# Recurrent attention and a two-layer mixer on one core: the last batch's u transposed by TensorE, and a new group order

## The chip, the cores and the metric

One core of a Trainium2 chip. The metric is device time in microseconds (us), the median of five runs. A separate profiled execution gives the trace; its times are microseconds from the start of its span. The engines are called PE or TensorE (matmul; PEld is its weight load), DVE or VectorE, ACT or ScalarE, POOL or GpSimd, and SP or SyncE. A "q" after an engine's name (ACTq, SPq) is its sequencer, which issues DMAs.

## The reference

Four batches, eight heads of 48, 768 steps, all in float32. First a gated linear recurrence, then a mixer along the sequence with rank 32 and a two-layer MLP (384 to 1536 to 384):

```python
for t in range(S):
    state = alpha[:, :, t, :, None] * state + einsum('bhd,bhe->bhde', k[:, :, t], v[:, :, t])
    y[:, :, t] = einsum('bhd,bhde->bhe', q[:, :, t], state)
x = y.transpose(0, 2, 1, 3).reshape(B, S, H * D)
h = x.transpose(0, 2, 1) @ U @ V          # along the sequence, rank 32
u = x + h.transpose(0, 2, 1)
out = u + maximum(u @ w_ch1, 0) @ w_ch2
```

## The kernel before, in words

Each batch is cut into six chunks of 128 steps. The kernel holds four kinds of work for a batch, in this order of dependence.

*The attention of a chunk.* alpha, k, q and v are loaded by SyncE's queue (L370 for batches 0 and 1, L377 for 2 and 3). ScalarE takes the log (lt, L400 or L583). TensorE sums it along the steps (L415 to L424, or L590 and L592). ScalarE makes the exponentials aa and ai (L431, L432, L600, L601) and tot. VectorE or GpSimd multiplies: rk = k times ai, rq = q times aa (L446, L612). Both are transposed to kt and qt. In batches 0 to 2 TensorE does it through PSUM (L459, L632) with a copy by ScalarE (L324) or VectorE (L326). In batch 3 a DMA transpose on ScalarE's queue does it (L623), 12 of them: the set TRD names batch 3's six chunks. TensorE then makes the scores (L486, L653), VectorE masks them (pm, L497, L663), and TensorE adds the state's part and the chunk's part (L560 and L567, or L710 and L712) to a bank that is copied to xb. A state st is carried from chunk to chunk (L518 or L676, then L545 or L699 and L531 or L687). Batches 0 and 1 (PAIR) use another split of heads and steps, in six units of the same kind.

*The mixer.* utx is xb against U for all six chunks (L727), copied once. Each chunk then gets one matmul against V (L758), and VectorE adds xb to it: ub (L759). For the first layer, u must stand transposed, as uT. Batch 0 (XT) builds it on TensorE from xb directly (L746, L749). Batches 1 and 2 transpose ub on TensorE, two chunks and six 128x128 tiles at a time (L774), and VectorE or ScalarE copies the bank to uT. Batch 3 (the tuple TRU) instead issues one DMA transpose per chunk on ScalarE's queue (L763).

*The first layer* (mlp1): for each half of the sequence and each of 12 column groups, three 128x384 matmuls (L801) and a ReLU copy to h1t by ScalarE (L811) or VectorE (L813).

*The second layer* (mlp2): for each chunk, 12 matmuls in three groups of four (L831), the sum with u on VectorE (L843), and the store by SyncE (L848).

*The order.* Nothing runs where it is written. Every step is recorded as an operation with its possible engines, its cost on each, what it reads and what it writes; 1035 in all. The long string TABLE then lists the operations by number, with a letter where an engine is chosen (P, A, V, G). `place` walks through TABLE with a model of the engines' clocks and gives out the buffers, and `run` emits the operations in that order, so each engine's queue is TABLE's order cut down to its own operations. In the head, `run` adds matmuls on a filler tile (L317) where the model has TensorE idle. An operation of mode "X" is a DMA transpose; `place` gives it a landing time, which is one of the two constants that the diff touches:

```python
if op.mode == "X":
    clock[eng] = t + cost
    end[op] = t + (4300.0 if dma > t + 800.0 else 2700.0) - self.LAT[eng]
    dma = max(dma, t) + 300.0
```

These numbers are not seen by the hardware. They matter for which buffer an operation gets and for the filler count.

Buffers come from pools: 36 for loads (io), three for kt, four for qt, three for uT, four for the stored rows (ou), and eight PSUM banks. All DMAs, the loads and stores of SyncE's queue and the transposes of ScalarE's queue, share eight completion semaphores in turn, so a DMA is not issued before an earlier one with the same semaphore has landed.

Of the kernel before, what the change touches and what calls it, by code (L numbers as in the profile page):

```python
# [39 lines left out]
class Plan:  # L40
# [47 lines left out]
    def place(self, table):  # L88

        names = {"P": "PE", "A": "ACT", "V": "DVE", "G": "POOL", "S": "SP"}  # L90
        self.order = []
        clock = dict(self.BEGIN)
        dma = port = 0.0
        mode = "F"
        end = {}
        lanes = []
        for x in table.split():
            op = self.ops[int(x.rstrip("PAVGS"))]
            eng = op.eng = names[x[-1]] if x[-1] in names else next(iter(op.engs))
            cost = op.engs[eng]  # L100
            t = clock.get(eng, 0.0)
            for d in op.deps:
                t = max(t, end[d] + (0.0 if eng == d.eng == "PE" else self.LAT[d.eng]))
            for b in op.bufs:
                if b.slot is None:
                    free = b.pool.free
                    at, b.idx = min((f, n) for n, f in enumerate(free) if f is not None)
                    b.slot = b.pool.slots[b.idx]
                    free[b.idx] = None
                    t = max(t, at)  # L110
            if eng == "POOL":
                t = max(t, port)
            if eng == "DVE" and op.port:
                t = max(t, port - self.PORT)
            queued = eng == "SP" or op.mode == "X"
            if queued and len(lanes) >= 8:
                t = max(t, lanes[-8])
            op.t = t
            if op.mode == "X":
                clock[eng] = t + cost  # L120
                end[op] = t + (4300.0 if dma > t + 800.0 else 2700.0) - self.LAT[eng]
                dma = max(dma, t) + 300.0
            elif eng == "SP":
                dma = max(dma, t + 500.0) + cost
                clock[eng] = max(t + 450.0, dma - 2300.0)
                end[op] = dma + (600.0 if op.deps else 1200.0)
            else:
                if eng == "PE" and op.mode != mode:
                    cost += self.SWITCH
                    mode = op.mode  # L130
                clock[eng] = end[op] = t + cost
                if eng == "POOL" or (eng == "DVE" and op.port):
                    port = end[op]
            if queued:
                lanes.append(end[op] + self.LAT[eng])
            for b in op.bufs:
                b.left -= 1
                b.last = max(b.last, end[op] + self.LAT[eng])
                if b.left == 0:
                    b.pool.free[b.idx] = b.last  # L140
            self.order.append(op)
        self.clock = clock
# [14 lines left out]


TABLE = """
61 69 73 201 224 157 204 160 65 62 64 63 179 66 182 227 161 162 206 184 183 67 164G 158G 165V 186G 1 159A 205 163 71 167 166 70 68 187V 169V 209G 188  # L160
189 168A 230 190A 191A 180A 207 170 173 171 174 172 74 72 192 211 4 181G 208G 228 77 202G 231G 75 81 78 213A 229 185 194 76 195 175 210 176 203A 212V
177 178A 247 214 233 193 196 235A 197 217 218 250 268 215 251 232G 252 79 254G 216 198 234 199 271 236V 200V 219 82 80 83 84 6 85 225G 237 253 226A 272
273 256 220 274 258A 93 5 19 89 21 23 255V 275G 240 257 221 3 248G 259A 241 222 239 242 238 25 27 31 277 260 29 33 35 91 13 17 249A 279A 86 51 97 87
263 88 15 276V 243 278 264 270A 269G 2 261 8 7G 20G 244 280A 245 284 262 285 265 286 22G 281 388 246A 90 39 92 43 37 41 95 282 24G 9 11 432 223A 266
283 267V 391 287 26G 45 10V 394 288A 53 94 49 295 292 298 392 393 410 12V 289 290 304 435 307 291V 305 299 293 296 30G 301 101 47 294V 436 300A 308
297A 302 96 413 306A 32A 28A 415 414 318 316 36G 418G 34G 309V 303V 342 343A 344 322 326 327A 323V 345V 416 319A 59 57 105 55 103 99 320 324 340 346
332 325V 347V 321V 395G 18G 348 328 354 352 438 437 341A 100 14A 98 102 106 356 353A 455 349V 317V 355V 329V 396V 417G 330 420 397 399V 350 16A 331A
422A 107 398 389G 411G 390G 0 336 314 315A 337V 357V 400A 351A 104 310 419 338 421V 311V 339V 312 334 404 38A 333A 40A 42A 423 401 313V 109 424 405 406
402 403 108 110 412G 426 44G 458 460 461 52A 335A 50G 113 368 358 363 427 478 408 373 425 440V 428 439G 111 459 46A 48A 481 434G 429G 430 359 409V 482
433A 431A 483 484 58A 499 56A 54A 407G 60G 442 369 448 441 449 374 364 502 444V 443V 450G 486G 451 463V 457G 504 503 462G 360 445 446 361 465 370 488  # L170
365 456A 485V 447 505 467A 490A 506G 471 487 464 453 508 366 489V 371 117 372 115 112 491 466A 507G 468 118 114 119 472 454A 493 509 473G 375 479A 510A
480G 494 452G 511A 618 474 470 495 500A 378 512 469 620 501G 621 475V 492 515 379 476 637 622 496G 497 516 624G 514 513 498A 626 517G 639 518 625V 627
477V 380 641 623 519A 640 642 116 520 125 120 367 127 134 129 121 130 123 122 126 133 145 135 628V 629V 630 381 383 631 632 124 521A 657 524 528 530
384 522 659 619G 644G 643G 661 662 525 531 534 385 536 523 660 526 664G 638G 663G 658G 529 532 535 537 633 646 645 538 533V 527A 554 552 386 648A 539V
582 666 647A 553V 668A 584 558 570 652 555V 634 583V 559V 585V 665 540 132 131 141 137 387 128 653 541V 580 560 544 545V 376 667A 377 153 142 581A 571A
697 649 669 671 561V 546 548 562 670 651 650 549A 572 677 566 586 547A 563A 574 699 654V 567V 587A 717 679 564 672 550 702 680 565A 700 701 551V 683V
673 576 542 681 577A 578 556 573V 557V 575V 568 685 655 719 675 832 569V 676V 682 543A 674G 684G 703G 834 579A 836 635 686 603 720 835 837 721 687A 604
636V 704V 723V 656V 839G 678G 598 599 706 705 605 725 724G 838G 707V 727V 722 688A 708A 709 689 841 867 711 710 691 606 726 600 593 692 698G 728A 849
840 693 690 601 149 382 602 136 147 729 588 851 869 870 872 885 138 146 589 712 139 694G 731 713 695 594 595 715 730 714G 871 696A 718A 732 590 716V
733V 842 843 873G 591 844 734 607 921 887 608 903 735A 853 744 742 738 609 743 745 890 889 852 833A 750 875 888 751 739 892G 748 610 746 749 855G 891G  # L180
613 856G 736 752 611 140 592 747V 753V 143 905 847 614 845 794 615 894 906 893 908 858 737 907 850A 740 846 795V 874G 741V 848V 596 784 800 758 759V
616 785V 151 150 801V 854 857 754 923 862 780 790 768 796 755A 925 876 863 781V 797A 778 772 791A 779V 773V 769V 764 760 788 864G 910G 909V 765V 924
761A 926 756 144 155 154 148 152 757A 912 789V 868G 877 895 859 896 878 879 897 766 762 927V 860 798 767A 763A 880 886G 881 928V 911 929 861 802 883
803 770 898 786 792 882G 904G 799A 930 771A 884A 793V 899 787V 900V 774 865 807 776 916 782 866A 777A 775V 783A 917 362 617 156 913 931 914 915 901 817
902A 812 933 932 919 818 922G 918G 934 827 920A 935A 828 936 804 937A 944 941 945 805 942 813 950 946 808 938 953 951 939 819 943 940 947 822 823 814
824 954 948 806 612 597 952 955 829 809 949 962 970 956 830 815 825 968 960 972 820 963V 958 964 969A 957V 965A 986 990 984 816 831 821 987V 991V 959A
985A 961V 976 810 982 983A 971A 994 978 992 996 979A 973V 966 980 981V 988 967V 977A 989A 974 1004 997V 1002 975V 1003A 998 1019 1024 1000 1005 995A
993V 1001A 999A 1020 1021 1006 1014 1025 1015 1009 1026 1016 1007 1022 1010 1011 1023 1008 826 1027 1017 1029 811 1028 1012 1032 1018 1013 1030 1031
1033 1034
"""  # L190


# [5 lines left out]
def kernel(  # L198
# [31 lines left out]

    PAIR = (0, 1)
    TRD = {(3, c) for c in range(NC)}
    TRU = (3,)
    XT = (0,)
    P = Plan()
    nc.scalar.preload_act_table_set("natural_log_exp_and_others")
# [148 lines left out]
    def xk(b, xb, c):  # L385
        return [(xb, c, 0), (xb, c, 1)] if b in PAIR else [(xb, c)]
# [334 lines left out]
    def stage_mix(b, xb, ub, uT):  # L721
# [34 lines left out]
        for c in range(NC):  # L756
            hb = Buf(bank)
            P.add({"PE": mm(DM)}, lambda e, c=c, hb=hb: nc.tensor.matmul(hb()[:, 0:DM], lhsT=vm_sb[:, c * C : (c + 1) * C], rhs=utx(), start=True, stop=True), r=[utx, ("vm", c // NT)], w=[hb])  # L758
            P.add({"DVE": 465}, lambda e, c=c, hb=hb: nc.vector.tensor_tensor(ub()[:, c, :], xb()[:, c, :], hb()[:, 0:DM], op=ALU.add), r=[hb] + xk(b, xb, c), w=[(ub, c)])  # L759
            if b in TRU:  # L760
                P.add(
# [141 lines left out]
```

## Time and profile before

| | before |
|---|---|
| runs (us) | 164.51, 163.67, 163.83, 164.35, 163.97 |
| median | 163.97 |
| profiled execution: its time, its span | 164.51, 162.7 |
| granted TensorE clock, mean | 1.00 |
| busy us: PE, weight loads, DVE, ACT, POOL | 153.1, 101.4, 117.1, 92.4, 60.2 |
| first L801 (first layer of batch 0) issued at | 28.62 us |
| DMA transposes: q of batch 3, median to landing | 6 of 4.6 us |
| DMA transposes: k of batch 3, median to landing | 6 of 3.6 us |
| DMA transposes: u of batch 3, median to landing | 6 of 3.1 us |
| TensorE's transposes of u in batches 1 and 2 (L774) | 36, no idle time before them |

A busy time is the union of an engine's instructions. A matmul's end is modelled and lies behind its stream of columns, so two matmuls that follow each other overlap in the rows; what a matmul costs is the distance from its start to the next one's. In the chain of work that ended last each piece is cut to the time in which it held up the rest. In a row of a timeline, "x30" is a run of 30 equal instructions, with its first start and the time to its last end.

### The profile page before, as it was taken

The numbers are of one execution on the slowest core, as the hardware profiler recorded it, in microseconds if no ns is written. First come the engines' busy times: TensorE is split into PE (matmuls) and PEld (weight loads), VectorE is DVE, ScalarE is ACT, GpSimd is POOL, SyncE is SP. The second block draws the span as 40 slices with busy tenths as digits, with TensorE's granted clock in tenths as the row PEclk, the third lists the DMA queues.
The fourth block names the chain that finished last, engine by engine and source line by source line (L and its number), as shares of the span: only waits on it lengthen the run. The fifth ranks groups of instructions, "written<-read, shape, count | busy, mean of one in ns | idle before, by whom it ended". The sixth has DMA issues, their size and how long they took to land.

```text
span 162.7 us, 4418 instructions
## 1 busy us (share of the span) xinstructions
PE 153.1 (94%) x1663; PEld 101.4 (62%) x1663; DVE 117.1 (72%) x255; ACT 92.4 (57%) x232; POOL 60.2 (37%) x94
## 2 busy tenths in 40 slices
PE   7789989999999999999999999997999997999992
PEld 2446867666676876765677666664657564666662
DVE  6379997486947998988798979887995437443241
ACT  4798999758798767635977465453353100453000
POOL 3197654538348675500078246332241000000000
PEclk9999999999999999999999999999999999999999
DMA  5999899999999898998997569999920097200072
GB/s 125 285 292 277 215 278 291 334 256 342 360 273 266 174 227 164 235 197 165 208 229 149 131 154 240 254 177 187 237 53 0 0 163 209 69 0 0 12 283 98
DMA packets 92198, 30.97 MB, mean 190 GB/s; under 512 B 85872, under 2 KB 92144, under 8 KB 92176
## 3 DMA queue, kind: packets, MB, share of 16 engines
q1 hardware_dynamic: 83152, 28.52, 72.3%
q10 hardware_dynamic: 9024, 2.16, 7.6%
q8 instruction: 13, 0.21, 0.5%
q14 instruction: 9, 0.07, 0.2%
HBM read 23.79 MB, written 4.72 MB: 175 GB/s over the span
## 4 chain that ended last, share of the span: by engine, by line
PE 73%; DMA 13%; SPq 6%; ACT 2%; issue 2%; DVE 2%; POOL 1%; DVEq 0%; POOLq 0%; ACTq 0%
PE ps L831 25%; PE ps L801 25%; DMA qt<-rq 6%; SPq L370 6%; DMA io<-in_k_dram 4%; DMA uT<-ub 3%; PE ps L653 2%; PE ps L632 2%; PE ps L459 2%; PE ps L567 2%; PE ps L486 1%; PE ps L712 1%; PE ps L758 1%; PE ps L590 1%; PE ps L774 1%
## 5 line engine op out<-in xcount | busy, mean ns | idle before, releaser
L831 PE MATMUL ps<-w_sb,h1t 128*128 128x384 bf16 (+2 forms) x300 | 53.7, 319 | 0.0
L801 PE MATMUL ps<-uT,w_sb 128*128 128x384 bf16 x288 | 50.2, 326 | 1.1 <-DMA uT<-ub 1.1
L811 ACT ACTIVATE h1t<-ps 128x384 bf16<-128x384 f32 x44 | 20.8, 496 | 31.3 <-PE ps L801 20.8
L801 PEld LDWEIGHTS <-w_sb 128*128 128x128 bf16 x288 | 27.2, 98 | 18.1 <-issue 1.5
L831 PEld LDWEIGHTS <-h1t 128*128 128x128 bf16 x300 | 27.0, 97 | 14.7 <-issue 0.3
L813 DVE TENSOR_SCALAR h1t<-ps 128x384 bf16<-128x384 f32 x52 | 26.8, 552 | 12.0 <-PE ps L801 12.0
L843 DVE TENSOR_TENSOR ou<-ub,ps 128x384 f32<-128x384 bf16 (+2 forms) x19 | 9.7, 528 | 11.4 <-PE ps L831 11.3
L497 DVE TENSOR_TENSOR pm<-ps,maskp 128x512 bf16<-128x512 f32 x24 | 15.9, 682 | 1.7 <-PE ps L486 0.8
L663 DVE TENSOR_TENSOR pm<-ps,maskc 128x512 bf16<-128x512 f32 x24 | 15.5, 684 | 2.0 <-PE ps L653 1.6
L687 POOL TENSOR_TENSOR st<-sm,tot 128x384 bf16<-128x384 f32 x6 | 5.2, 870 | 24.1 <-DMA io<-in_q_dram 12.4
L446 POOL TENSOR_TENSOR rk<-io,ai 128x384 bf16<-128x384 f32 x11 | 10.1, 926 | 10.0 <-DMA io<-in_v_dram 4.9
L759 DVE TENSOR_TENSOR ub<-xb,ps 128x384 bf16<-128x384 bf16 x18 | 8.8, 548 | 4.2 <-PE ps L758 4.2
L612 POOL TENSOR_TENSOR rq<-io,aa 128x384 bf16<-128x384 f32 x9 | 8.5, 949 | 8.5 <-ACT aa L601 5.8
L324 ACT COPY qt<-ps 128x512 bf16<-128x512 bf16 x14 | 9.6, 687 | 2.0 <-PE ps L632 1.1
L600 ACT ACTIVATE ai<-ps 128x384 bf16<-128x384 f32 x12 | 5.9, 501 | 5.0 <-PE ps L592 4.2
L324 ACT CAST xb<-ps 128x384 bf16<-128x384 f32 x14 | 6.6, 478 | 3.5 <-PE ps L712 1.7
L328 POOL CAST rw<-io 64x384 bf16<-64x384 f32 x14 | 7.7, 556 | 1.7 <-DMA io<-in_v_dram 0.9
L601 ACT ACTIVATE aa<-ps 128x384 bf16<-128x384 f32 x12 | 5.8, 497 | 3.8 <-DVE ub L759 1.7
L612 POOL TENSOR_TENSOR rk<-io,ai 128x384 bf16<-128x384 f32 x8 | 7.3, 916 | 1.9 <-PE ps L653 1.1
L328 POOL CAST w_sb<-io 128x384 bf16<-128x384 f32 x11 | 5.5, 505 | 6.2 <-DMA io<-in_moe_w_ch_dram 6.1
L400 ACT ACTIVATE lt<-io 128x384 bf16<-128x384 f32 x12 | 6.2, 525 | 2.4 <-DMA io<-in_alpha_dram 2.3
L446 DVE TENSOR_TENSOR rq<-io,aa 128x384 bf16<-128x384 f32 x7 | 4.8, 691 | 3.3 <-DMA io<-in_q_dram 3.2
(124 smaller groups left out, 259.6 us busy)
## 6 DMA issues: line engine op xcount, KB each, us to landing
io<-in_alpha_dram SPq DMA_DIRECT2D x24, 192.0 KB, 3.9
io<-in_k_dram SPq DMA_DIRECT2D x24, 192.0 KB, 4.5
io<-in_v_dram SPq DMA_DIRECT2D x24, 192.0 KB, 4.1
io<-in_q_dram SPq DMA_DIRECT2D x24, 192.0 KB, 4.4
io<-in_moe_w_ch_dram SPq DMA_DIRECT2D x24, 192.0 KB, 4.5
out_dram<-ou SPq DMA_DIRECT2D x23, 192.0 KB, 2.9
out_dram<-ou SPq DMA_DIRECT2D x1, 128.0 KB, 1.7
v_in<-in_moe_V_dram SPq DMA_DIRECT2D x1, 96.0 KB, 3.5
```

The lines of the kernel that those rows point to most:

```text
L324: nc.scalar.copy(dst, src)
L328: nc.gpsimd.tensor_copy(dst, src)
L370: lambda e: nc.sync.dma_start(t().rearrange("p (h j) d -> p h (j d)", j=2), src[b, hs, sl, :].rearrange("h (p j) d -> p h (j d)", j=2)),
L446: eng.tensor_tensor(jh(dst()[:, :, 0:D]), raw(a), jh(x()), op=ALU.mult)
L497: nc.vector.tensor_tensor(dst, s2, maskp.to_broadcast([C, 2, 2, C]), op=ALU.mult)
L612: eng.tensor_tensor(dst()[:, :, 0:D], a(), x(), op=ALU.mult)
L663: nc.vector.tensor_tensor(pm()[:, :, par, :], s2, maskc.to_broadcast([C, HP, C]), op=ALU.mult)
L801: nc.tensor.matmul(hb()[:, 0:TW], lhsT=w1_sb[:, ct, jt * 128 : (jt + 1) * 128], rhs=uT()[:, ct, tt * TW : (tt + 1) * TW], start=(ct == 0), ...
L811: nc.scalar.activation(dst, hb()[:, 0:TW], AF.Relu)
L813: nc.vector.tensor_scalar_max(dst, hb()[:, 0:TW], 0.0)
L831: nc.tensor.matmul(hb()[:, 0 : hi - lo], lhsT=h1()[:, jt, c * C : (c + 1) * C], rhs=w2_sb[:, jt, lo:hi], start=(jt == 0), stop=(jt == NJ - ...
L843: nc.vector.tensor_tensor(ou()[:, lo:hi], base()[:, c, lo:hi], hb()[:, 0 : hi - lo], op=ALU.add)
```

## The change

Three places change. TRU becomes empty, so batch 3's u takes the same path as that of batches 1 and 2: three groups of six TensorE transposes and three copies from PSUM in place of six DMA transposes. The number of operations stays 1035. The landing times that `place` gives a DMA transpose are longer. And TABLE is another order throughout, from the first load on, with other engines chosen for many copies and products. The 12 DMA transposes of batch 3's q and k stay on ScalarE's queue.

```diff
-                end[op] = t + (4300.0 if dma > t + 800.0 else 2700.0) - self.LAT[eng]
+                end[op] = t + (5000.0 if dma > t + 800.0 else 3800.0) - self.LAT[eng]
...
 TABLE = """
-61 69 73 201 224 157 204 160 65 62 64 63 179 66 182 227 161 162 206 184 183 67 164G 158G 165V 186G 1 159A 205 163 71 167 166 70 68 187V 169V 209G 188
...
-1033 1034
+69 65 61 201 157 179 63 64 62 160 204 162 165V 73 66 67 71 77 159A 161 164G 158G 167 182 169V 184 163 206 183 207 224 205 75 166 173 70 168V 186V 174
...
+1034
 """
...
     TRD = {(3, c) for c in range(NC)}
-    TRU = (3,)
+    TRU = ()
     XT = (0,)
```

The order's effect on single engines, counted in the instruction lists of the two kernels: VectorE takes 59 of the 96 h1t copies (52 before), 11 of the kt copies from PSUM (8), 7 of the qt copies (4), three more of the st products of batches 1 and 2, 11 of the uT copies (8); ScalarE makes one of the two vm copies and batch 0's utx copy. In batch 3 ScalarE's transposes come in the order of chunks 0, 2, 1 and 3 mixed, 5, 4; before it was 0, one of 2, 3, 1, the other of 2, 4, 5.

## The prediction

> **What bounds the kernel now.** I read the page first, for shares; then busy time by windows, for who is full where; then TensorE's waits and the chain, for what stops it; then TensorE's timeline at those stops.
>
> ```profile
> span 162.7 us, 4418 instructions
> ...
> PE 153.1 (94%) x1663; PEld 101.4 (62%) x1663; DVE 117.1 (72%) x255; ACT 92.4 (57%) x232; POOL 60.2 (37%) x94
> ```
>
> The same, by windows (PE, weight loads, DVE, ACT, POOL, granted clock, DMA share, GB/s):
>
> ```profile
> 28.60:108.00 79.40, 79.38 (x908) 53.97 (x907) 66.29 (x133) 54.14 (x144) 38.55 (x55) 1.00 0.99 228
> 108.00:113.50 5.50, 4.46 (x47) 2.75 (x45) 3.85 (x9) 2.54 (x7) 2.41 (x3) 1.00 1.20 180
> 113.50:122.50 9.00, 8.49 (x97) 5.48 (x92) 8.63 (x17) 3.69 (x8) 3.30 (x5) 1.00 0.68 142
> 122.50:131.00 8.50, 8.50 (x88) 5.26 (x86) 4.32 (x9) 1.91 (x4) 0.00 (x0) 1.00 0.09 21
> 131.00:136.20 5.20, 4.10 (x26) 2.32 (x25) 2.53 (x6) 0.00 (x0) 0.00 (x0) 1.00 0.95 158
> 136.20:159.80 23.60, 23.54 (x156) 14.68 (x156) 9.26 (x19) 5.83 (x13) 0.00 (x0) 1.00 0.28 93
> ```
>
> From 28.6 us, the first matmul of the first MLP layer, TensorE is full except around 112, 122 and 136 us. Its waits and the chain name the same culprit, DMA transposes:
>
> ```profile
> PE ps L653 <- DMA qt<-rq: 1.6, 2, 1.0
> PE ps L801 <- DMA uT<-ub: 1.1, 1, 1.1
> ```
>
> ```profile
> 106.76 5.88 DMA qt<-rq
> 112.77 0.85 PE ps L653 x24
> ...
> 117.97 4.05 DMA qt<-rq
> 122.16 0.40 PE ps L653 x8
> ...
> 131.63 4.38 DMA uT<-ub
> 136.15 0.97 PE ps L801 x5
> ```
>
> A matmul's end is modelled late, so I count issue to issue; the chain's merged rows give 0.162 us for a 128x384 matmul (0.49 for three). Then:
>
> ```profile
> 106.69 5.04 PE L801 MATMUL ps<-uT,w_sb 128*128 128x384 bf16 x30
> 121.25 0.40 PE L653 MATMUL ps<-qt,kt 48*128 48x128 bf16 x8
> 130.98 4.06 PE L831 MATMUL ps<-w_sb,h1t 128*128 128x384 bf16 x24
> ```
>
> Thirty matmuls fill 4.86 us, to 111.55; the next starts at 112.77: 1.2 lost. The eight score matmuls fill 0.19, to 121.44; the next start at 122.16: 0.7 lost. Twenty-four fill 3.89, to 134.87; the next starts at 136.15: 1.3 lost. Together **3.2 us**. That is all the change can win after 28.6 us, save 0.15 us at each return from a score group to full-width matmuls (24 score matmuls hold TensorE 0.85 us in the chain, 8 hold 0.40).
>
> **Part 1: batch 3's u by TensorE.** Six DMA transposes leave ScalarE's queue (issued 129.00 to 137.11, landing after 2.4 to 5.4 us); three groups of six TensorE transposes and three evictions come. The rows for this in batches 1 and 2 are "PE ps L774", 0.34 us for six and 0.67 for twelve: 18 cost **+1.0 us**, all on the path since TensorE is full there. The three evictions (0.55 us on VectorE twice, 0.80 on ScalarE once) should be covered. I follow the tightest hand-over in the changed order. L758 of chunk 2 is issued; its sum on VectorE starts 0.36 us later (128.06 to 128.42 in the trace) and lasts 0.55, so it is there after 0.91. TensorE meanwhile has L758 itself (0.16), four L831 (0.65) and the transposes of chunks 0 and 1 (0.34), so it asks for that sum after 1.15. The transposes of chunks 2 and 3 then take 0.34, a matmul's tail about 0.16, the eviction 0.55: uT is there after 1.05, while TensorE does those transposes, one L758 and four L831 (1.15). L801 starts with 0.1 to spare, and the 1.3 us wait goes. If this cover fails by one VectorE instruction, it costs 0.5. SyncE's later stores reused the semaphores of the six transfers; they have until the end and gain nothing.
>
> The Trainium skill speaks against this part: "TensorE: Matmul & The Clock Gate", Part 4, gives a 128x128 TensorE transpose about 275 ns in one kernel's context; by that figure 18 would cost an estimated 4.95 us, and the sum below would come out 2.9 us above the kernel before. The rows above give 56 ns from issue to issue, at a granted clock of 1.00, and the measurement decides.
>
> **Part 2: q and k of batch 3 stay 12 DMA transposes on ScalarE's queue; the new order places their users later.** Landings in the loaded stretch (97 to 112 us) took 4.13, 4.54, 4.11, 4.76, 6.28 and 5.88 us. Before, the score group of chunks 1 to 3 waited for chunk 2's q, loaded last and transposed at 106.76. In the new order ScalarE waits for chunk 0's result (L712), copies it (0.48) and issues the last four at 1.2 us each, so the last is issued about 4.4 us after that L712. TensorE has 18 groups of L801 (0.49 each), one L676 and one L590/L592 in that interval, 9.2 us: 4.8 remain to land. Four of six rows fit, two miss by 1.1 and 1.5: I take **0.4** (0 to 1.5) instead of 1.2. Of chunks 4 and 5 the last transpose waits for a qt buffer that chunk 1's L710 reads last; from there to its scores TensorE has six groups of L831 and 1.1 us of small groups, 5.0, against a flight of 4.05 at that place before: 0 to 0.5, I take **0.1** instead of 0.7. Behind that wait on ScalarE stand the xb copies of chunks 2 and 1, which TensorE needs only for L727. Loads can stand behind a transpose too: a load or store reuses the semaphore of an earlier transfer, and "SPq L848 <- DMA qt<-rq" is 3.0 us in SyncE's waits. In the new order it is chunk 1's k and q loads that wait for chunk 0's two transposes; all loads for the first score group still come before ScalarE reaches their transposes, by my stepping some 2 us. One return from scores fewer in the order: **-0.15**.
>
> **Part 3: the head.** The same work stands before the first L801 in both orders, but VectorE gets three more kt copies (0.42), one more rk product (0.69), one more xb copy (0.55), one qt copy fewer (0.73): +1.9 us, and it is full there:
>
> ```profile
> 12.00:16.00 4.00, 3.66 (x66) 2.56 (x65) 3.88 (x9) 3.48 (x10) 3.28 (x5) 1.00 1.04 275
> 16.00:20.00 4.00, 3.77 (x72) 3.23 (x70) 3.89 (x9) 3.83 (x11) 2.15 (x3) 1.00 0.86 222
> 20.00:24.00 4.00, 3.58 (x78) 2.70 (x76) 4.00 (x10) 3.88 (x8) 2.65 (x7) 1.00 1.06 274
> ```
>
> Against it: its first product waited until 8.18 us for a q loaded seventh; that q is now fourth, and its aa (1.3 us after a lt that starts at 5.3) allows it at about 7.1 (-1.1); one vm copy and the utx copy move to ScalarE (-1.1), which sheds three kt copies, one rw copy and one xb copy (-2.7, +0.7 for a qt). Stepping through both lists with these durations I get L801 at about 28.9 against 28.6: **+0.3** (-0.5 to +1.5).
>
> **Part 4: the rest of the order.** Every group moves, so any hand-over may miss. Counted by engine, the new order puts work on VectorE: seven h1 evictions more (0.55 each), three kt (0.42), three qt (0.4 to 0.73), one rk product, three st products, three uT evictions, against one vm and one utx copy fewer: about +9.6 us, from 117 to 127. Before, full stretches of VectorE cost TensorE nothing (66.29 of 79.40 busy, TensorE 79.38). I take **+0.5** (0 to 2.5) for new gaps; below nothing is excluded, as TensorE has no gap there to give back.
>
> Sum: +1.0 - 3.2 + 0.4 + 0.1 - 0.15 + 0.3 + 0.5 = -1.05 us. The profiled execution took 164.51 us, span 162.7 (1.8 lie around it); it is the slowest of the five runs, 0.54 above their median of 163.97. Taking the sum from the median: **162.9 us**.
>
> **Rivals.** (a) *Nothing new waits*: 3.2 gone, 1.0 paid, 0.15 gained, head as before: -2.35, so 161.6. For it: all the waits found have one cause, and four of the six landings seen would be in time. Against: four engines with handovers of 0.1 us to spare. (b) *The transposes wait again*: chunk 3's last transpose rows in at 5.9 to 6.3 us and one wait of 1.2 stays: -1.05 + 0.8 gives about 163.7, no change. For it: two of six rows. (c) *Slower: VectorE becomes the bound*. Place: batch 2's attention, 60 to 96 us, where windows of 4 us (read as above) sum to 31.7 busy of 36; one h1, one kt, two qt, one rq and two st more, one rk and one xb fewer, make that 34.1. Price: if the 4.3 us it idled there were all forced on it, the 2.4 come whole to TensorE, and with 0.6 more in the head: -1.05 - 0.5 + 2.4 + 0.6 = +1.45, so 165.4. It decides from the point where VectorE costs TensorE 1.6 us more than I allow in the head. Against it: VectorE's long waits were for TensorE's results (12.0 us for L801's, 11.3 for L831's), slack that a later VectorE can use.
>
> **How the numbers follow.** Chances: my forecast 0.42, (a) 0.19, (b) 0.15, (c) 0.24. A measurement of this kernel tells about 0.3% from no change, 0.5 us. Faster: (a) and nine tenths of the forecast's, 0.57. Within: the other tenth and two thirds of (b), 0.14. Slower: (c) and what (b) leaves, 0.29. Range: below, (a)'s 161.6 less 0.1; above, into (c) up to 165.2, so that about a tenth is out on each side. The likeliest case alone runs from 162.1 to 163.6.
>
> **What would show it.** Right: no L763; L774 48 to 54 in count, no wait of L801 on uT over 0.2; L653's waits on qt under 0.6 in all; first L801 at 28.1 to 30.1; TensorE busy throughout to about 1.2 us sooner. Wrong: L653 waiting over 1.5, first L801 past 30.5, or TensorE waiting on VectorE lines (L663, L497, L759) for more than 1.6 between 30 and 125 us. The whole fails if the transposes' rows are much over 0.34 for six.

## The result and the profile after

| | before | after |
|---|---|---|
| median of all runs beside each other (us) | 164.51 (80 runs) | 163.54 (43 runs) |
| lowest and highest | 162.94, 165.84 | 162.21, 164.88 |
| ratio of after to before, 95 % interval | | 0.9955, 0.994 to 0.997 |
| profiled execution: its time, its span | 164.51, 162.7 | 164.44, 162.7 |

The changed kernel is faster, by 0.74 us after the ratio (0.5 to 1.0) and by 0.97 after the medians. A ratio leaves out executions that lie well above the fastest of their kernel, so it need not be the quotient of two medians. The single profiled execution shows none of this: its span is the same as before. That contradiction is what the experiments had to clear up.

The page of the changed kernel, first the shares:

```profile
span 162.7 us, 4458 instructions
...
PE 154.7 (95%) x1683; PEld 102.6 (63%) x1683; DVE 125.8 (77%) x274; ACT 85.3 (52%) x218; POOL 57.9 (36%) x92
```

VectorE has 8.7 us more to do (9.6 were forecast), ScalarE 7.1 less. By windows, cut at the new order's own stages (columns as before):

```profile
28.80:108.00 79.20, 78.13 (x899) 53.44 (x897) 69.58 (x139) 50.61 (x134) 35.48 (x51) 1.00 0.98 221
108.00:116.00 8.00, 7.05 (x66) 4.27 (x63) 7.37 (x15) 3.61 (x10) 2.29 (x4) 1.00 1.11 165
116.00:124.60 8.60, 8.60 (x88) 5.49 (x82) 7.12 (x15) 0.56 (x2) 3.02 (x4) 1.00 0.74 140
124.60:129.90 5.30, 5.30 (x75) 3.61 (x74) 3.44 (x6) 2.04 (x5) 1.27 (x2) 1.00 0.20 74
129.90:135.75 5.85, 5.85 (x48) 3.54 (x47) 3.15 (x6) 1.28 (x2) 0.00 (x0) 1.00 0.28 104
135.75:159.90 24.15, 24.12 (x165) 15.20 (x163) 13.09 (x26) 4.36 (x10) 0.00 (x0) 1.00 0.18 66
```

From 116 us on TensorE is full: the waits at chunk 5's scores and at uT are gone. It lacks about 1 us in each of the first two windows. TensorE's waits and the chain of waits name both:

```profile
PE ps L459 <- DVE rq L446: 1.2, 2, 1.0
...
PE ps L653 <- DMA kt<-rk: 1.0, 1, 1.0
```

```profile
52.32 1.04 DVE rq L446
53.40 0.40 PE ps L459 x4
...
110.16 5.54 DMA kt<-rk
115.75 0.40 PE ps L653 x8
```

TensorE's timeline at the places where the kernel before stood still:

```profile
109.21 5.04 PE L801 MATMUL ps<-uT,w_sb 128*128 128x384 bf16 x30
114.18 0.62 PE L653 MATMUL ps<-qt,kt 48*128 48x128 bf16 x16
115.75 0.40 PE L653 MATMUL ps<-qt,kt 48*128 48x128 bf16 x8 [0.95 <-DMA kt<-rk]
...
124.59 0.62 PE L653 MATMUL ps<-qt,kt 48*128 48x128 bf16 x16
125.14 1.15 PE L801 MATMUL ps<-uT,w_sb 128*128 128x384 bf16 x6
```

```profile
135.12 0.81 PE L831 MATMUL ps<-w_sb,h1t 128*128 128x384 bf16 x4
135.77 1.64 PE L801 MATMUL ps<-uT,w_sb 128*128 128x384 bf16 x9
```

Four L831 fill 0.65 us: 135.12 to 135.77, so the first L801 on u starts without a wait. The second score group (124.59) has none either. Chunk 3's scores, the last eight of the first group, stand for its k: the last of the sixteen before them is issued at 114.58, they start at 115.75, 1.17 us later, where 0.05 is the usual step. And there is a new one, of 1.12 us beyond the usual step: the transposes of batch 1 unit 4's rq (L459, 53.40) wait for VectorE's product (L446).

### The profile page after: what moved, and what is told of

It reads as the page before. It is cut to its first block, busy times and chain, and to the rows that moved or that the text cites. A ratio compares the mean times of both kernels' runs of the same rounds, so it can differ in the third digit from the quotient of the medians.

```text
span 162.7 us, 4458 instructions
## 1 busy us (share of the span) xinstructions
PE 154.7 (95%) x1683; PEld 102.6 (63%) x1683; DVE 125.8 (77%) x274; ACT 85.3 (52%) x218; POOL 57.9 (36%) x92
## 4 chain that ended last, share of the span: by engine, by line
PE 75%; DMA 11%; DVE 5%; ACT 3%; issue 2%; SPq 1%; POOL 1%; ACTq 0%; POOLq 0%; DVEq 0%
PE ps L831 26%; PE ps L801 24%; DMA kt<-rk 3%; PE ps L459 3%; DMA qt<-rq 3%; DMA io<-in_alpha_dram 3%; DMA io<-in_v_dram 2%; PE ps L567 2%; DVE rq L446 2%; PE ps L486 2%; PE ps L632 2%; PE ps L653 2%; PE ps L518 2%; PE ps L774 1%; PE ps L758 1%
## 5 line engine op out<-in xcount | busy, mean ns | idle before, releaser
L831 PE MATMUL ps<-w_sb,h1t 128*128 128x384 bf16 (+2 forms) x300 | 53.1, 319 | 0.0
L801 PE MATMUL ps<-uT,w_sb 128*128 128x384 bf16 x288 | 50.9, 326 | 0.0
L801 PEld LDWEIGHTS <-w_sb 128*128 128x128 bf16 x288 | 26.8, 98 | 16.2 <-DVE uT L326 0.2
L831 PEld LDWEIGHTS <-h1t 128*128 128x128 bf16 x300 | 27.2, 98 | 15.2 <-issue 0.3
L813 DVE TENSOR_SCALAR h1t<-ps 128x384 bf16<-128x384 f32 x59 | 30.0, 551 | 6.6 <-PE ps L801 6.4
L811 ACT ACTIVATE h1t<-ps 128x384 bf16<-128x384 f32 x37 | 16.8, 500 | 16.7 <-PE ps L801 16.5
L324 ACT CAST xb<-ps 128x384 bf16<-128x384 f32 x13 | 5.9, 480 | 14.2 <-PE ps L712 14.2
L328 POOL CAST w_sb<-io 128x384 bf16<-128x384 f32 x16 | 7.8, 504 | 5.3 <-DMA io<-in_moe_w_ch_dram 5.1
L446 POOL TENSOR_TENSOR rk<-io,ai 128x384 bf16<-128x384 f32 x7 | 6.4, 912 | 8.9 <-ACT ai L431 6.3
L687 POOL TENSOR_TENSOR st<-sm,tot 128x384 bf16<-128x384 f32 x4 | 3.3, 828 | 16.3 <-DVE sm L699 16.3
L324 ACT COPY qt<-ps 128x512 bf16<-128x512 bf16 x11 | 7.7, 698 | 2.5 <-PE ps L459 1.9
L317 PE MATMUL ps<-filler 128*128 128x512 bf16 x17 | 7.0, 543 | 1.2 <-DVE filler L251 1.2
L612 POOL TENSOR_TENSOR rq<-io,aa 128x384 bf16<-128x384 f32 x8 | 7.3, 915 | 1.3 <-POOL rk L612 1.0
L400 ACT ACTIVATE lt<-io 128x384 bf16<-128x384 f32 x12 | 6.2, 526 | 2.8 <-DMA io<-in_alpha_dram 2.8
L446 POOL TENSOR_TENSOR rq<-io,aa 128x384 bf16<-128x384 f32 x6 | 6.1, 1008 | 4.4 <-ACT aa L432 4.0
L326 DVE CAST xb<-ps 128x384 bf16<-128x384 f32 x11 | 6.1, 553 | 1.7 <-PE ps L712 1.5
```

The costliest lines, as they stand in the source:

```text
L324: nc.scalar.copy(dst, src)
L328: nc.gpsimd.tensor_copy(dst, src)
L446: eng.tensor_tensor(jh(dst()[:, :, 0:D]), raw(a), jh(x()), op=ALU.mult)
L612: eng.tensor_tensor(dst()[:, :, 0:D], a(), x(), op=ALU.mult)
L801: nc.tensor.matmul(hb()[:, 0:TW], lhsT=w1_sb[:, ct, jt * 128 : (jt + 1) * 128], rhs=uT()[:, ct, tt * TW : (tt + 1) * TW], start=(ct == 0), ...
L811: nc.scalar.activation(dst, hb()[:, 0:TW], AF.Relu)
```

## The experiments

Steps of the order are named here by batch (b), chunk (c) or unit (u) and result: scores (L653) and y (a chunk's output, L710 and L712); M1 with its column group jt (three L801) and M2 (four L831); hu (a chunk's L758), TU (its transposes on TensorE, L774) and TRU (its DMA transpose, L763); trk and trq (the transposes L459 of rk and rq). "Control" is the changed kernel run in the same series; series 2 and 3 have none, so their kernels are set against the controls of other series; the kernel before had medians of 164.59, 164.72, 164.27, 164.12 and 164.34 us in the five series.

| series | kernel | median, runs | ratio to before, 95 % interval |
|---|---|---|---|
| 1 | after_again (control) | 163.45, 12 | 0.9922, 0.9895 to 0.9950 |
| 1 | rq_first | 163.50, 9 | 0.9918, 0.9879 to 0.9956 |
| 1 | c3_scores_late | 162.84, 7 | 0.9898, 0.9862 to 0.9935 |
| 1 | u_pe_old_order | 164.12, 12 | 0.9981, 0.9951 to 1.0012 |
| 2 | both | 162.93, 6 | 0.9893, 0.9859 to 0.9927 |
| 2 | double_tu | 164.33, 12 | 0.9982, 0.9957 to 1.0006 |
| 2 | u_dma_new_order | 167.28, 6 | 1.0127, 1.0075 to 1.0180 |
| 2 | old_fixed | 164.57, 12 | 0.9996, 0.9973 to 1.0020 |
| 3 | cover_late | 163.61, 12 | 0.9962, 0.9938 to 0.9987 |
| 3 | c3_pe | 163.41, 12 | 0.9961, 0.9933 to 0.9988 |
| 3 | cover_c3_pe | 164.07, 12 | 0.9990, 0.9962 to 1.0018 |
| 4 | after_third (control) | 163.31, 12 | 0.9925, 0.9894 to 0.9956 |
| 4 | c3_scores_late2 | 162.88, 12 | 0.9935, 0.9911 to 0.9959 |
| 4 | gp_first | 162.36, 12 | 0.9924, 0.9894 to 0.9953 |
| 4 | gp_first_late | 162.77, 12 | 0.9931, 0.9906 to 0.9957 |
| 5 | after_fourth (control) | 163.52, 12 | 0.9947, 0.9920 to 0.9974 |
| 5 | gp_first2 | 162.86, 10 | 0.9910, 0.9877 to 0.9943 |

### Part 1 alone, and its price

**u_pe_old_order.** The order before, with only the tail behind batch 3's utx rearranged around TensorE's transposes.

```diff
-    TRU = (3,)
+    TRU = ()
 TABLE, from utx's copy to the first L801 of batch 3:
-c2 hu, c1 hu, M2, c4 hu, TRU c2, M2, c0 hu, c5 hu, M2, TRU c1, TRU c0, c3 hu, four M2, TRU c4, TRU c5, two M2, TRU c3
+c0, c1, c2 hu, two M2, c3 hu, M2, TU c0-1, c4 hu, M2, TU c2-3, c5 hu, two M2, TU c4-5, three M2
```

> The kernel before, its order untouched up to the copy of batch 3's utx; from there to the first L801 of batch 3 its u is transposed by TensorE (three groups of L774, two copies on VectorE, one on ScalarE) and no DMA transposes are issued for u. That is part 1 of the change alone. Theory: 18 transposes cost 1.0 us, the wait of 1.3 us at L801 goes, the waits at 112 and 122 us stay: 0.3 us faster than the kernel before, 0 to 0.5. Rival 1: the transposes are dearer in their context than 56 ns; at the 275 ns of the Trainium skill (TensorE: Matmul & The Clock Gate, Part 4) the kernel would be an estimated 3.6 us slower. Rival 2: the stores that stood beside the DMA transposes took 4.8 to 5.1 us instead of 1.9; without them something behind the stores gains more, 1 us or over.

Its time was 164.12 against 164.59, 0.5 us less (0.3 by the ratio), with an interval that just includes none. TensorE's timeline of it, at the hand-over of u:

```profile
132.97 0.50 PE L774 MATMUL ps<-ident,ub 128*128 128x128 bf16 x6
133.30 2.11 PE L831 MATMUL ps<-w_sb,h1t 128*128 128x384 bf16 x12
135.25 1.95 PE L801 MATMUL ps<-uT,w_sb 128*128 128x384 bf16 x11
```

Six transposes take 0.33 us, twelve L831 1.95, and L801 follows at once: 1.27 of wait gone for 1.0 of transposes. The trace and the time agree with the theory; the two rivals (3.6 slower, 1 or more faster) lie outside the interval. The two score waits stayed, but at 0.8 and 0.6 us where the kernel before had 1.2 and 0.7, in an order that is the same up to there: a first sign that one profile does not fix the length of such a wait.

**double_tu.** The 18 transposes done twice into the same place.

```diff
-for cc in (c - 1, c):
+for cc in (c - 1, c) * (2 if b == 3 else 1):
```

> The changed kernel with each of batch 3's 18 TensorE transposes of u (L774) done twice into the same place, so 36 instead of 18 there; the result is the same. It measures the price of the 18 by itself. Theory: 56 ns from issue to issue, 1.0 us more than the changed kernel (0.7 to 1.2), no new wait, all of it on the path. Rival 1: the 275 ns that the Trainium skill gives in context (TensorE: Matmul & The Clock Gate, Part 4): an estimated 5 us more. Rival 2: TensorE is not the bound at that place; then under 0.4 us more.

TensorE's timeline at those groups:

```profile
133.89 1.50 PE L774 MATMUL ps<-ident,ub 128*128 128x128 bf16 x24
135.23 0.33 PE L758 MATMUL ps<-utx,vm_sb 128*128 128x384 bf16 x1
...
138.65 0.83 PE L774 MATMUL ps<-ident,ub 128*128 128x128 bf16 x12
139.32 0.98 PE L801 MATMUL ps<-uT,w_sb 128*128 128x384 bf16 x5
```

24 take 1.34 us and 12 take 0.67: 56 ns each, 1.0 us for 18, and the median is 0.8 to 1.0 above the controls' 163.31 to 163.52 of the other series. The 275 ns that the Trainium skill gives ("TensorE: Matmul & The Clock Gate", Part 4) are not what a transpose in a run of them costs here.

**u_dma_new_order.** Part 1 undone in the new order.

```diff
-    TRU = ()
+    TRU = (3,)
 TABLE, from utx's copy to the first L801 of batch 3:
+c0, c1, c2 hu, each ub followed by its TRU, one M2, c3 hu, ub, TRU, two M2, c4 and c5 the same, two M2
```

> The changed kernel's order with u by six DMA transposes on ScalarE's queue again, each right behind its ub, with chunks 0 to 2 first and the four groups of batch 2's second layer that this order has left all ahead of the first L801 of batch 3; part 1 undone, the rest of the new order kept. Theory: the third transpose can be issued 3.4 us after the first L758 and lands about 3 us later; TensorE has some 3.6 us of work in that interval, so L801 waits 2 to 3.5 us on uT, and 1.0 of transposes is saved: 1.0 to 2.5 us slower than the changed kernel, so 0.2 to 1.5 slower than the kernel before. Rival: the transposes land in 2.4 us with an empty DMA system and TensorE loses under 1.2: then the time is within 0.3 us of the changed kernel, and the tensor path wins nothing by itself.

It was slower than forecast: by the ratio 2.1 us above the kernel before, where 0.2 to 1.5 were expected. Its wait for uT, and two windows (columns as above):

```profile
PE ps L801 <- DMA uT<-ub: 3.6, 1, 3.6
```

```profile
134.00:137.60 3.60, 0.11 (x1) 0.00 (x0) 1.57 (x3) 0.00 (x0) 0.00 (x0) 0.96 0.88 216
137.60:140.90 3.30, 3.23 (x11) 1.59 (x12) 0.00 (x0) 0.00 (x0) 0.00 (x0) 0.52 0.50 132
```

L801 lost 3.7 us, a little over the 2 to 3.5 expected, and behind the wait the granted clock was 0.52: the next matmuls came 0.32 us apart instead of 0.16 and cost another 1.5. So the new order and part 1 belong together. It uses the second layer's groups earlier, and without TensorE's transposes it has nothing to put in front of uT. In the old order the same part was worth 0.3 to 0.5.

### Is the new order needed?

**old_fixed.** The old order with u by TensorE, and the two score groups that waited moved later by hand.

```diff
-c2, c3, c1 scores, b2 M1 jt6, jt4, jt10, ... c2 y, M2, M1 jt8 ... c4, c5 scores, c3 y, M2, M2, c4 y, M2, c5 y, M2
+c3, c1 scores, b2 M1 jt6, jt4, c2 scores, jt10, ... M2, M1 jt8, c2 y ... c4 scores, c3 y, M2, M2, c5 scores, c4 y, M2, M2, c5 y
```

> The old order with u by TensorE (as in u_pe_old_order) and two more moves by hand: batch 3's chunk-2 scores go behind two groups of L801 (with the masks and chunk 2's outputs in step), chunk 5's scores behind two groups of L831, because TensorE waited 0.8 to 1.2 and 0.6 to 0.7 us there for their DMA transposes. It asks if the new order as a whole is needed. Theory: both waits fall to under 0.3 us in all, two more returns from scores cost 0.15 each: 1.0 to 1.4 us faster than u_pe_old_order, about 162.9, as good as the new order or better. Rival: chunk 2's later scores keep its kt and qt longer, the transposes of chunks 4 and 5 are issued later by as much, and the wait at chunk 5's scores grows to 1 us or over: under 0.5 us faster than u_pe_old_order.

164.57: no gain over u_pe_old_order, whose interval overlaps this one. Both score waits are gone from the trace, but the timelines of TensorE, of ScalarE's queue and of VectorE show what came instead:

```profile
120.47 0.65 PE L801 MATMUL ps<-uT,w_sb 128*128 128x384 bf16 x3 [0.70 <-ACT h1t L811]
```

```profile
117.70 2.17 ACTq L623 DMA_TRANSPOSE qt<-rq  x1
119.93 0.49 ACT L811 ACTIVATE h1t<-ps 128x384 bf16<-128x384 f32 x1 [3.18 <-DVE h1t L813]
```

```profile
114.22 2.48 DVE L663 TENSOR_TENSOR pm<-ps,maskc 128x512 bf16<-128x512 f32 x4
...
117.08 0.55 DVE L612 TENSOR_TENSOR rq<-io,aa 128x384 bf16<-128x384 f32 x1
```

The rival's time came true (under 0.5 us faster), but not its reason. Chunk 5's transpose of q takes the buffer of chunk 2, whose outputs end at 117.1; ScalarE's queue stands until 117.64 for the product rq itself, which VectorE makes behind four masks in a row, and then the issue takes 2.17 us where it took 1.20 before. ScalarE's ReLU copies stand behind it, idle for 3.18 us, and TensorE waits for one of them. Why that issue is so long, the trace does not say. Two local repairs in the old order are not the new order.

Of the change's three places the landing times were not run alone. With the old ones under the new TABLE, `place` gives the same number of filler matmuls and every buffer but one (chunk 4's rq in batch 3 takes another of its three).

### The two waits that were left

**after_again.** 

> The changed kernel once more, for a second trace. Theory: the two waits of TensorE that are left in its trace belong to the order, so they come again at the same places, 1.1 us at the transposes of batch 1's unit 4 (L459, near 53 us) and 0.8 to 1.5 us at the scores of batch 3's chunk 3 (L653, near 115 us), and the time is 0.4 to 0.6 % under the kernel before. Rival: they belong to that one execution, which lies 0.9 us above the median of its kernel; then at least one of them is under 0.4 us here, and the execution is shorter by as much.

Both waits came again, 1.12 and 1.21 us, in an execution of 164.52, the slowest of its runs.

**rq_first.**

```diff
-b1 u0 xb (VectorE), b1 u4 rq (VectorE)
+b1 u4 rq (VectorE), b1 u0 xb (VectorE)
```

> The changed kernel with one VectorE step moved: batch 1 unit 4's product rq ahead of unit 0's copy xb. In the trace that product starts at 52.24 and takes 1.11 us beside GpSimd's own product (52.02 to 52.93), where 0.55 is usual, and TensorE stands 1.1 us for it. Theory: it starts 0.47 us earlier, mostly ahead of GpSimd's, and ends 0.6 to 1.0 us earlier; the wait at L459 falls from 1.1 to 0.1 to 0.5 us, and the kernel is 0.5 to 1.0 us faster than the changed one, about 0.9 % under the kernel before. Rival: the chunk-3 scores of batch 3 wait for a DMA transpose whose time is set by loads and not by TensorE, so that wait grows by what is won here: the wait at L459 goes, the one at L653 grows from 1.2 to about 2, and the time is within 0.2 us of the changed kernel.

In its trace the wait fell from 1.12 to 0.12 us and the span from 162.7 to 161.7, as the theory has it; the wait at chunk 3's scores was 1.03, not 2, against the rival's reason. But the median stayed where it was, as the rival had it.

**c3_scores_late.**

```diff
-c2, c1, c3 scores, b2 M1 jt11, jt4, M2 c1, ...
+c2, c1 scores, b2 M1 jt11, jt4, M2 c1, c3 scores, ...
```

> The changed kernel with batch 3's chunk-3 scores (and their mask) moved behind two groups of L801 and one of L831, 1.6 us of TensorE's work, so that the 1.2 us wait for their k falls away. Theory: the wait goes to 0, one more return from scores costs 0.15, and the kernel is 0.8 to 1.1 us faster than the changed one. Rival: chunk 3's later mask delays its state and the transposes of chunks 4 and 5, which wait for buffers, so their scores (L653 near 124 us, no wait now) stand instead: 0.5 to 1.2 us there and a time within 0.3 us of the changed kernel.

The wait is gone, no other grew, and the median is 0.6 below the control, less than forecast.

**both.** 

> The changed kernel with both single moves together: batch 1 unit 4's product rq ahead of the copy xb on VectorE, and batch 3's chunk-3 scores and mask 1.6 us of TensorE's work later. Moved alone, the first took TensorE's wait at L459 from 1.12 to 0.12 us in the trace but left the median where it was (163.50 against 163.45); the second took the median to 162.84. Theory: what the first wins is given back at the chunk-3 scores, whose k is timed by DMA, so with those moved too it counts: 0.5 to 1.0 us below the second alone, about 162.1. Rival: the loads and the DMA transposes of batch 3 set the time of more than that one group, so the first stays worth nothing here either: 162.6 to 163.0, with a new TensorE wait on a DMA somewhere from 80 to 125 us.

162.93: the product ahead is worth nothing here either. Yet no wait on a DMA appeared, so the rival's reason is wrong as well. In this trace TensorE still lost 0.70 us at L459: VectorE's product rk, in the same place, took 1.27 us beside GpSimd's in place of rq, and the copy xb behind it, which TensorE waited for, was late by as much.

**cover_late** and **cover_c3_pe** cover the wait on TensorE's side; **c3_pe** takes away the DMA transposes of chunk 3.

```diff
-b1 u4 trk, u4 trq, b0 M2 c0, ..., u3 trk, b0 M2 c3, ...
+b1 u4 trk, b0 M2 c0, M2 c3, u4 trq, ..., u3 trk, ...
```

```diff
-    TRD = {(3, c) for c in range(NC)}
+    TRD = {(3, c) for c in range(NC) if c != 3}
```

> The changed kernel with batch 3's chunk-3 scores and mask late (as in c3_scores_late) and, on TensorE, the transposes of batch 1 unit 4's rq (L459) moved behind two groups of L831, 1.3 us of work that needs nothing new. In the traces of this order the wait there is 0.16, 0.70, 1.09 or 1.12 us, by whether VectorE's products fall beside GpSimd's. Theory: the wait differs between executions, so its cover wins about its mean, 0.4 to 0.8 us, below c3_scores_late (162.84): 162.2, and the runs lie closer together. Rival: as moving the product ahead won nothing (both: 162.93), the later stages swallow it here too: 162.7 to 163.0, and then a wait must be longer behind 57 us than in c3_scores_late.

> The changed kernel with chunk 3 of batch 3 taken out of TRD: its q and k are transposed by TensorE (L641 and L642, eight transposes, 0.45 us, two copies on ScalarE) in place of the last two of six DMA transposes that stand in one row. Theory: DMA transposes in a row wait for each other; in the six traces of this order so far the last one took 5.4 to 5.6 us while the first took 3.2 to 6.1. With two fewer the transposes of chunk 1 land sooner (flights under 4.6 instead of 5 to 5.8), the wait of 0.9 to 1.2 us at L653 goes, and 0.45 is paid: 0.3 to 0.7 us faster than the changed kernel, about 162.9. Rival: the flights are long because of the loads beside them; then chunk 1's q still takes 5 us or more, and lands after its scores are due, so a wait of 0.3 us or over stays and the gain is under 0.3.

> Both of the above in one: unit 4's rq transposes behind two more groups of L831, and chunk 3's q and k by TensorE. Theory: 0.4 to 0.8 us below c3_pe, about 162.3, and no wait of TensorE over 0.4 us between 30 and 125 us. Rival: what is won at 53 us is lost at the next hand-over that a DMA times; then it equals c3_pe within 0.2.

The cover failed: 163.61 where c3_scores_late had 162.84, and 0.66 on top of c3_pe. TensorE and ScalarE in the timelines of cover_c3_pe:

```profile
55.55 0.42 PE L486 MATMUL ps<-qt,kt 48*64 48x128 bf16 x16 [0.64 <-ACT qt L324]
```

```profile
53.70 0.74 ACT L324 COPY qt<-ps 128x512 bf16<-128x512 bf16 x1 [1.08 <-PE ps L459]
54.47 0.42 ACT L439 ACTIVATE tot<-ps,offb 128x4 f32<-128x4 f32 x2
54.77 0.73 ACT L324 COPY qt<-ps 128x512 bf16<-128x512 bf16 x1
```

ScalarE's copy of unit 4's qt waits for the transposes that were moved, unit 3's copy queues behind it, and the scores L486 wait for them. Both profiles with the cover lost the same: 40.56 us from the first to the 73rd L801, 0.8 to 0.9 more than the 39.6 to 39.8 of the profiles with next to no wait at L459, while the wait it replaced comes and goes. In c3_pe chunk 1's q was there after 3.22 us (5.1 to 5.5 in the profiles of the changed kernel), and the wait at L653 had gone, as the theory said; its time was that of the changed kernel all the same. That q is now the fourth in its row, and the fourth in the changed kernel took 3.4 to 5.6, so one flight does not settle what makes them long. (The expectation's 5.4 to 5.6 for the last flight is too narrow: it was 6.3 in after_again and 4.6 in c3_scores_late.)

**after_third**, **after_fourth.** The controls gave the answer.

> The changed kernel as it is, a control beside the next three, and a third profile of its own. Theory: in the profile the transposes of batch 1 unit 4's rq (L459, 53 us) wait 1.0 to 1.2 us and chunk 3's scores (L653, 115 us) 0.7 to 1.2, and the profiled execution is among the slowest of its runs, as in both profiles so far (164.44 and 164.52 against medians of 163.5). Rival: one of the waits is absent this time and the execution lies at the median.

> The changed kernel as a control again. In three profiles the wait at L459 (53 us) was 1.12, 1.12 and 0.03 us, by whether GpSimd's product rk of unit 3 had started at 49.3 or at 48.9. Theory: it is one or the other here too, never between 0.3 and 0.9; where it is 1.1 the execution lies above the kernel's median, where it is nil below. Rival: the wait is spread evenly, and its place in the order of runs says nothing.

In after_third the wait at L459 nearly vanishes (0.08), the one at L653 falls to 0.51, and the span is 161.0. VectorE and GpSimd at 50 us, in the first profile of the changed kernel and then in this one:

```profile
49.59 0.91 DVE L531 TENSOR_TENSOR st<-sm,tot 128x192 bf16<-128x192 f32 x1
...
52.24 1.11 DVE L446 TENSOR_TENSOR rq<-io,aa 128x384 bf16<-128x384 f32 x1
```

```profile
49.37 0.91 POOL L446 TENSOR_TENSOR rk<-io,ai 128x384 bf16<-128x384 f32 x1 [1.87 <-DMA io<-in_k_dram]
52.02 0.91 POOL L446 TENSOR_TENSOR rq<-io,aa 128x384 bf16<-128x384 f32 x1 [1.74 <-ACT aa L432]
```

```profile
49.58 0.44 DVE L531 TENSOR_TENSOR st<-sm,tot 128x192 bf16<-128x192 f32 x1
...
51.75 0.55 DVE L446 TENSOR_TENSOR rq<-io,aa 128x384 bf16<-128x384 f32 x1
```

```profile
48.89 0.91 POOL L446 TENSOR_TENSOR rk<-io,ai 128x384 bf16<-128x384 f32 x1 [1.39 <-ACT w_sb L324]
52.02 1.06 POOL L446 TENSOR_TENSOR rq<-io,aa 128x384 bf16<-128x384 f32 x1 [2.21 <-ACT aa L432]
```

A k load that lands half a microsecond later starts GpSimd's rk at 49.37 instead of 48.89. VectorE's st, which begins just after, then takes 0.91 instead of 0.36 to 0.44, so VectorE's rq starts after GpSimd's (52.02) instead of before it and takes 1.11 instead of 0.55. Half a microsecond of DMA becomes 1.1 of TensorE. after_fourth was the other case again (1.12), though not for the reason its expectation gives: GpSimd's rk waited there for TensorE until 50.63, and the next st, at 50.88, was held up. With the other kernels that have this place unchanged, nine profiles gave 1.12, 1.12, 0.08, 1.12, 1.12, 0.10, 1.09, 1.12 and 0.16 us, and nothing between. What tells the two cases apart in all nine is not when rk starts but what it meets: in the six long ones a st of VectorE begins 0.04 to 0.29 us behind it and takes 0.84 to 1.09 us; in the three short ones the st begins ahead of it or over 0.6 us behind, and no st takes more than 0.51.

**What the profiles add up to.** I take from each profiled execution's time its two waits (at L459 without, at L653 with the usual step) and the distance of its first L801 from 28.84 us (the 0.08 of after_third is the difference of the stages from the first to the 73rd L801, 39.69 and 40.73, taken from 1.12):

| kernel | its time | first L801 | at L459 | at L653 | left |
|---|---|---|---|---|---|
| after | 164.44 | 28.84 | 1.12 | 1.17 | 162.15 |
| after_again | 164.52 | 28.85 | 1.12 | 1.21 | 162.18 |
| after_third | 162.73 | 28.84 | 0.08 | 0.51 | 162.14 |
| after_fourth | 164.29 | 29.25 | 1.12 | 0.60 | 162.16 |
| rq_first | 163.55 | 29.07 | 0.12 | 1.03 | 162.17 |
| gp_first | 162.33 | 28.99 | 0 | 0 | 162.18 |
| gp_first2 | 163.28 | 28.73 | 0.35 | 0.88 | 162.16 |
| c3_scores_late | 163.17 | 28.49 | 1.12 | 0 | 162.40 |
| c3_scores_late2 | 162.69 | 29.04 | 0.10 | 0 | 162.39 |
| both | 163.40 | 29.10 | 0.70 | 0 | 162.44 |
| gp_first_late | 163.86 | 30.29 | 0 | 0 | 162.41 |
| c3_pe | 163.87 | 28.72 | 1.12 | 0 | 162.87 |
| double_tu | 165.05 | 28.77 | 1.09 | 0.88 | 163.15 |

The rest is constant to 0.04 us over the four profiles of one kernel, and the edits move it by what they cost: later scores 0.25, chunk 3 on TensorE 0.7, eighteen more transposes 1.0. So the execution times of the changed kernel are 162.15 plus two waits that come and go plus the head. Its medians of 163.3 to 163.5 hold some 1.2 to 1.4 us of the 2.3 that its first profile showed (an estimate from the table). This fits rq_first (it takes away a wait that many executions don't have, and that returns by another product) and c3_pe (0.7 paid for a wait of 0.5 to 1.2).

**gp_first, gp_first2.** Take the collision away, not the wait: unit 4's rq goes to GpSimd, which stood idle there.

```diff
-b1 u4 rq (VectorE), ..., b1 u3 rk (GpSimd)
+b1 u4 rq (GpSimd), b1 u3 rk (GpSimd)
```

> The changed kernel with one product moved between engines: batch 1 unit 4's rq goes from VectorE (52.2 us in the trace, beside GpSimd's product, 1.11 us) to GpSimd, ahead of its product rk of unit 3, where GpSimd waits 1.9 us for a load anyway. Unit 4's q lands at 48.6, so the product is there at 49.5, 3 us before TensorE asks for it. Theory: the wait at L459 is gone in the profile (under 0.2), VectorE has 0.55 us less, and the median falls by what this wait costs in ordinary executions; as moving the product ahead on VectorE did not lower the median (163.50 against 163.45), I expect 0 to 0.4 us. Rival: the wait is in ordinary executions as it is in the profile, and rq_first only shifted it: then 0.8 to 1.1 us faster than the changed kernel.

> The kernel of gp_first once more beside the changed kernel: its median was 0.95 us lower (162.36 against 163.31), while the ratios to the kernel before were equal (0.9924 and 0.9925), so the gain is undecided. Theory: the wait of 1.1 us at L459 stands in about half of the changed kernel's executions and in none of this one's: 0.4 to 0.9 us faster in both the median and the ratio. Rival: what is won is given back at chunk 3's scores, timed by a DMA: under 0.2 us, and in the profile the wait there is 1.5 us or more.

GpSimd's rows in gp_first, the moved product first:

```profile
48.36 0.91 POOL L446 TENSOR_TENSOR rq<-io,aa 128x384 bf16<-128x384 f32 x1 [0.72 <-ACT w_sb L324]
49.23 0.92 POOL L446 TENSOR_TENSOR rk<-io,ai 128x384 bf16<-128x384 f32 x1
```

The medians are 0.95 and 0.66 below their controls; all 22 runs have a median of 162.52 against 163.44 of the controls' 24. The ratios show 0.0 and 0.4 %. It has the lowest median of all versions and is ahead of the kernel before in both series; by the ratios both and c3_scores_late lie lower, within the intervals. How far it is ahead of the changed kernel is less sure than that it is not behind. The collision is not gone for good either: in gp_first2 the moved product started only at 49.66, GpSimd's rk behind it met VectorE's rk (1.26 us), and 0.35 us were lost at L459. The wait at L653 was 0.88 there, against the rival's 1.5 or more.

**c3_scores_late2, gp_first_late.** 

> The kernel of c3_scores_late once more, beside the changed kernel on the same chip, since seven runs decided it. Theory: 0.4 to 0.9 us faster than the changed kernel (0.6 before), no wait at L653 in the profile. Rival: the difference was the chip's or the draw's; under 0.2 us.

> Both: unit 4's rq early on GpSimd, and batch 3's chunk-3 scores late. Neither of the two waits that were left can then occur. Theory: the sum of the two single effects, 0.6 to 1.0 us below the changed kernel, and the runs lie within 1.2 us of each other (the changed kernel's within 2.2). Rival: the full 2.2 us that the two waits hold in the profile: about 161.3.

The first repeated its gain (0.4). The two edits together are no faster than gp_first alone: the later scores cost 0.25 always, for a wait that is often short. The profiled head of gp_first_late was 1.3 us late, with the fourth lt (L400) at 12.10 where the other profiles of this order have 9.9 to 10.9; 0.4 us of this is a later alpha load, the rest was not followed. The head scatters in all these kernels, and that was not studied.

## Why the prediction was right or wrong

The direction, the mechanism and most terms held; 162.9 was 0.6 too low.

- **The base is the step that failed.** "It is the slowest of the five runs ... Taking the sum from the median: 162.9." The profiled execution's 164.51 was not an outlier: it is the median of 80 runs, and the five series put the kernel before at 164.1 to 164.7. From it the same sum gives 163.46; 163.54 was measured, and that this is so close is partly luck, as the next point shows.
- **The size of the move**, -1.05 forecast, is just outside the interval of the ratio (-0.5 to -1.0, in the middle -0.74; -0.97 by the medians). Two terms were mis-sized inside it; by the estimate above, which leaves some 0.4 us at L459 in a median execution, the first is too small and the second too large:
  - *The first score group, 0.4 left of 1.2.* It measured 1.17, 1.21, 0.51 and 0.60 in four profiles, mean 0.87. ScalarE's last issue came 4.4 to 5.1 us after it took up chunk 0's result (4.4 forecast), and the last flight took 5.5 to 6.3. I had read six flights as independent draws, four of six in time. But the transfer that counts is the sixth in a row, and it was among the slow ones in all four profiles, as the last two were before (6.28, 5.88). The 1.2 it replaces is itself one profile's: the same wait was 0.8 in u_pe_old_order.
  - *New gaps, 0.5.* There is one, at 53 us, of 0.1 or 1.1 and nothing between; beside it only the small ones at 86 and 90 us, which fewer stalls elsewhere outweigh.
- **+1.0 for the transposes**: 1.0 by the doubling. **-0.15 for one return from scores fewer**: not measured alone; the runs that add one (c3_scores_late) paid 0.25 for it.
- **-1.3 at uT and -0.7 at chunk 5's scores**: both gone, with the hand-over of 0.1 to spare holding in every profile that has this tail (12.05 us from the 217th L801 to the last in each).
- **The head, +0.3**: 28.84 against 28.62, +0.2; it scatters by more than that.
- **Rival (c)** named the right engine and the wrong place. From 60 to 96 us TensorE lost 0.4 more (0.1 at 86 and 0.3 at 90 us), not 2.4; the 1.1 us at 53 us came from a collision between two engines, not from a full VectorE. **Rival (b)** is what one sees in two of four profiles. **Rival (a)** would have needed both waits to be nil; after_third, closest to it of the changed kernel's profiles, ran 162.73.
- The mark "L653's waits on qt under 0.6" was put on the wrong tensor: q was in time, chunk 3's k was the last.

## What to carry to other kernels

One profile is one execution: before a wait in it is priced, look if its length is bistable, by two or three more profiles of the same kernel, and take the base from many runs. Where DMA transposes are queued in a row, take the flight of the one that is waited for (here the sixth), not the mean of all. A wait behind a slow instruction is better removed at its cause (here the two engines' products side by side) than covered at the waiter, where the cover pushes back whatever follows.

## What the runs showed of the hardware

- **VectorE and GpSimd hold each other up where VectorE reads two tiles of SBUF.** In the 19 traces a VectorE product of two SBUF tiles (rk, rq) took 0.55 us alone. When it started while a GpSimd instruction ran, it ended 0.41 to 0.44 us after that one's end (medians of the four kinds of row, 133 cases), and took up to 1.27. VectorE's masks, with one operand in PSUM, took 0.68 in either case (471 cases beside GpSimd, 441 without). GpSimd gave way too: where its product started in the middle of such a VectorE instruction, it took up to 1.31 instead of 0.91. The Trainium skill's "GPSIMD Engine Reference", section 1, states that the interfaces are shared with VectorE instructions that have two SBUF inputs; these rows agree and give the size.
- **DMA transposes in a row beside loads**: issued every 1.2 to 2.3 us, the sixth landed 5.5 to 6.3 us after its issue in the four profiles of the changed kernel and 4.2 to 5.7 in ten others that have this row; over all 14 the mean rises from 4.0 for the first to 5.4 for the sixth. In the next row (from 114 us on, as the last loads land) the first three took 2.4 to 3.6 and the fourth 3.5 to 3.9 in the changed kernel. Whether the row or the loads make them long was not separated: in c3_pe's row of four the flights fell from 6.4 to 3.2.
- **TensorE's clock fell to half in the one wait of 3.6 us** (u_dma_new_order, granted clock 0.52 in the 3.3 us behind it); the kernel before's stops of 1.2 and 1.3 us, counted from issue to issue, left it at 1.00. That wait was so paid twice, with 3.7 and 1.5 us.
